# Key masks moved to ScalarE, bfloat16 counts and a reordered turn 1 in a fused attention and expert kernel

## The chip, the cores and the metric

The kernel runs on one core of one Trainium2 chip. The metric is the device time of one execution in microseconds (us); lower is better. Before the change the kernel takes 670.79 us (median of three runs: 670.62, 670.79 and 671.94).

## What is computed

Clustered attention comes first, then a layer of experts on its output. A query sees only the keys of its own cluster, and every token goes to one expert.

```python
# q, k, v: (4 batches, 8 heads, 768 tokens, 64), float32; centroids: (8, 16, 64)
q_assign = argmax(q_n @ c_n.T)            # nearest of 16 centroids, per head
k_assign = argmax(k_n @ c_n.T)
mask     = q_assign[..., :, None] == k_assign[..., None, :]
scores   = where(mask, q @ k.T / 8, -1e9)
x        = softmax(scores) @ v            # reshaped to (3072, 512)
logits   = x @ w_gate                     # 8 experts
e        = argmax(logits);  g = softmax(logits)[e]
out      = g * (relu(x @ w1[e]) @ w2[e])  # w1: 512x1024, w2: 1024x512 per expert
```

## The kernel before

**Attention.** The work is cut into 16 pairs of heads, numbered 0 to 15 (`NPAIR`, four pairs for each batch). Within a pair, `score` (L384) runs for 2 halves of the queries times 6 tiles of 128 keys, 12 score tiles in all. Each score tile is one product of keys and queries and one product of the masks `MK` and `MQ` in bfloat16 (L379), accumulated in the same bank of PSUM, and then one exponential on ScalarE (L392). The mask product adds a huge number where key and query have the same cluster, and takes it away elsewhere. After all 12 tiles, `attend` (L400) multiplies the exponentials by v (L404), 24 product instructions, and ScalarE copies the two halves of the result out (`oT`, L411). VectorE adds up the exponentials (`acc`, L398).

The masks of pair n+1 are made during pair n by `prepare` (L469), in steps: `similar` (step 1) is the product with the centroids; `assign0`, `assign1` (step 2) and `assign2` (step 3) find the cluster on VectorE and end with a transposition into `ohT` (L348); `place` (L350) writes the masks. `place(n, 1)` is step 4 and makes the key mask `mk` from `ohT` with four VectorE instructions of 32 partitions x 384 (L361: times ksc2, plus kscn2, which are columns of 128 partitions); `place(n, 0)` is step 5 and makes the query mask `mq` with four ScalarE copies of the same shape (L359). `MK` and `MQ` have two buffers each, used alternately; the `ohT` buffer is single. The first pair's masks (n = 0) are made ahead of the loop.

What happens when is an order written out by hand. `at_pair(n, u, f)` (L771) queues a step after score tile u of pair n; u = 0 to 11 follow the score tiles, u = 12 and 13 follow the two halves of the product with v. Line 779 has the steps' places:

```python
for u, step in ((2 if n else 4, 1), (5, 2), (7, 3), (8, 4), (11, 5)):
    at_pair(n, u, prepare, n + 1, step)
```

In the trace each engine works through its instructions in the order of this code, so a step that waits on VectorE holds up every later VectorE step.

**Routing.** For each batch, `gate`, `choose`, `count` and `number` (L490 to L560) find each token's expert and its place in that expert's list. `count` (L535) is two TensorE products of 128x128 float32 weights (`lt_strict`, L539, and `ones_sq`, L540) with the 8 columns `last`. GpSimd writes the tokens to their places in `tokens_of` in DRAM (L554). The routing of the last batch runs inside expert turn 0.

**Experts.** There are 10 turns, numbered 0 to 9 (`EARLY` and `RANKED`, L28), each of 128 to 448 tokens of one expert. For turn s: `places(s)` (L653) reads a register and loads the tokens' places into `sf` by SyncE's DMA queue; `indices(s)` (L669) turns them into row numbers `gi` on VectorE; `gather(s)` (L678) fetches the rows `xg` by GpSimd; `weigh(s)` (L691, tile `xw`) multiplies them by weights on VectorE and writes them to DRAM; `take(s)` (L712, tile `xs`) reads them back in another arrangement; `turn_rows(s)` (L723, tile `xT`) transposes them. `layer1` (L895) and `layer2` (L999) multiply by w1 and w2 in seven products per block instead of eight (a Strassen-Winograd scheme), so VectorE makes sums of operands first: `x_sums` (tile `xc`), `w1_sums` (tiles `a0` to `a3`), `w2_sums` (tiles `v0` to `v3`), `h_sums` (tile `hs`). All of these sums go through `strassen`, so the profile has them on one line, L736. In `layer1` VectorE also adds two PSUM results (`add`, L874), and the last product of each half has to wait until the first of these additions has read its bank.

Inside a turn, `hook()` is called after each product, and `at(h1, i, f)` or `at(h2, i, f)` queues a step at hook i of layer 1 (hooks 0 to 6 belong to the first half of the columns, 7 to 13 to the second) or layer 2. Lines 1134 to 1182 hold this order. In turn 1, before the change, layer 1 has: hook 4, `indices(3)`, `gather(3)` and v1; hook 6, `weigh(2)` and then v3; hook 9, a2 of turn 2; hook 10, a1 of turn 2; and only after that the addition L874 of the second half. `ask` and `answer` (L622, L632) check the softmax sums once, in turn 3. SyncE issues nearly all DMAs of these turns from one queue, in order.

Of the kernel before, what the change touches and what calls it, by code (L numbers as in the profile page):

```python
# [8 lines left out]
F32 = mybir.dt.float32  # L9
# [24 lines left out]
def kernel(  # L34
# [11 lines left out]
    nc = tc.nc  # L46
# [73 lines left out]
    sums = rte.tile([P, NPAIR, HI], F32)  # L120

    lt_strict = consts.tile([P, P], F32)
    keep = consts.tile([P, E, TC], F32)
    ones_sq = consts.tile([P, P], F32)
    none = consts.tile([P, NPL // P, TR], F32)
# [11 lines left out]
    def routing_constants():  # L137
        nc.gpsimd.memset(none, float(NONE))
        nc.gpsimd.memset(none[:, :, 1:TR], 0.0)
        for e in range(E):  # L140
            nc.sync.dma_start(
                out=t_d[e * NPL : (e + 1) * NPL].rearrange("(p c) o -> p (c o)", p=P), in_=none.rearrange("p c o -> p (c o)")
            )
        nc.gpsimd.memset(lt_strict, 1.0)
        nc.gpsimd.affine_select(
            lt_strict, lt_strict, compare_op=ALU.is_gt, fill=0.0, base=0, pattern=[[1, P]], channel_multiplier=-1,
        )
        nc.gpsimd.memset(ones_sq, 1.0)
        nc.gpsimd.memset(keep, 1.0)
        nc.gpsimd.memset(keep[:, :, 0:1], 0.0)  # L150
        nc.gpsimd.memset(tg, 0.0)
        tok_a = iota("tok_a", [Q4, B, NQ, 4], [[S, B], [1, NQ], [S // 4, 4]], 0, NQ).rearrange("t b j a -> t b (j a)")
        for g in range(4):
            nc.gpsimd.tensor_copy(tg[Q4 * g : Q4 * (g + 1), :, :, 0], tok_a[:, :, TC * g : TC * (g + 1)])
        nc.gpsimd.memset(caps, 0.0)
        nc.gpsimd.memset(ranks, 0.0)
        for w, (cs, rs) in enumerate(((EARLY, range(len(EARLY))), (RANKED, RANKS))):
            for i, (c, r) in enumerate(zip(cs, rs)):
                nc.gpsimd.memset(caps[:, w, i : i + 1], float(c))
                nc.gpsimd.memset(ranks[:, w, i : i + 1], float(r))  # L160
        nc.gpsimd.tensor_copy(run, first_place)

    with tc.manual_schedule(), ExitStack() as actx:
# [186 lines left out]
        def place(n, w):  # L350
            t, m = OH[n], (MQ, MK)[w][n % 2]
            for h in range(2):
                for a in range(2):
                    g = 2 * w + h
                    dst = m[D * a : D * a + Q4, HS * h : HS * (h + 1)]
                    src = t[Q4 * g : Q4 * (g + 1), :]
                    if w == 0:

                        (nc.gpsimd.tensor_copy if n == 0 and h else nc.scalar.copy)(dst, src)  # L359
                    else:  # L360
                        nc.vector.tensor_scalar(  # L361
                            dst, src, scalar1=ksc2[Q4 * g : Q4 * (g + 1), a : a + 1],
                            scalar2=kscn2[Q4 * g : Q4 * (g + 1), a : a + 1], op0=ALU.mult, op1=ALU.add,
                        )
            if w == 0:
                OH.pop(n)

# [143 lines left out]
        def choose(b):  # L511

            lg = LG.pop(b)
            sc = rt.tile([P, TC, E], F32, name="sc")
            nc.vector.tensor_tensor(sc, lg, LMAX.pop(b).unsqueeze(2).to_broadcast([P, TC, E]), op=ALU.is_ge)
            nc.vector.scalar_tensor_tensor(
                sc, in0=sc, scalar=float(2 * E), in1=first_e[:, None, :].to_broadcast([P, TC, E]),
                op0=ALU.mult, op1=ALU.add,
            )
            mx2 = rt.tile([P, TC], F32, name="mx2")  # L520
            nc.vector.reduce_max(mx2, sc, axis=AX)
            sel = SEL[b] = rt.tile([P, E, TC], F32, name="sel")
            nc.vector.tensor_tensor(
                sel.rearrange("p e t -> p t e"), sc, mx2.unsqueeze(2).to_broadcast([P, TC, E]), op=ALU.is_equal,
            )
            pr = PR[b] = rt.tile([P, E, TC], F32, name="pr")
            nc.vector.tensor_tensor_scan(
                pr.rearrange("p e t -> p (e t)"), keep.rearrange("p e t -> p (e t)"),
                sel.rearrange("p e t -> p (e t)"), 0.0, op0=ALU.mult, op1=ALU.add,
            )  # L530

            last = LAST[b] = rt.tile([P, E], F32, name="last")
            nc.vector.tensor_copy(last, pr[:, :, TC - 1])

        def count(b):  # L535

            last = LAST.pop(b)
            cps = CPS[b] = BANK.pop()[:, 2 * P : 4 * P] if BANK else ps_m.tile([P, 512], F32, name="mps")
            nc.tensor.matmul(cps[:, 0:E], lhsT=lt_strict, rhs=last, start=True, stop=True)  # L539
            nc.tensor.matmul(cps[:, E : 2 * E], lhsT=ones_sq, rhs=last, start=True, stop=True)  # L540

        def number(b):
            pr, sel, cps = PR.pop(b), SEL.pop(b), CPS.pop(b)
# [194 lines left out]
        def x_sums(s):  # L738
            g = GR[s]
            b11, b12, b21, b22 = g["X"]  # L740
            n = g["T"]
            xc = xp.tile([P, 4 * T_MAX], F32, name="xc")
            X = [xc[:, i * n : (i + 1) * n].rearrange("p (b t) -> p b t", b=2) for i in range(4)]
            V = nc.vector
            strassen(V, X[0], b12, b11, ALU.subtract)
            strassen(V, X[1], b22, X[0], ALU.subtract)
            strassen(V, X[2], b22, b12, ALU.subtract)
            strassen(V, X[3], b21, X[1], ALU.subtract)
            g["XS"] = X

# [23 lines left out]
        for n in range(NPAIR):  # L774
            if n:
                at_pair(n, 2, sum_up, n - 1)
                at_pair(n, 4, rows, n - 1)
                at_pair(n, 4, store, n - 1)
            for u, step in ((2 if n else 4, 1), (5, 2), (7, 3), (8, 4), (11, 5)):
                at_pair(n, u, prepare, n + 1, step)  # L780
        for b in range(B - 1):
            n = HP * (b + 1)
# [59 lines left out]
    with tc.manual_schedule(), ExitStack() as ectx:  # L842
# [5 lines left out]
        seeded = pool("seeded", 3, space=PSUM)  # L848
        for _ in range(3):
            nc.tensor.matmul(  # L850
                seeded.tile([P, 512], F32, name="sbank"), lhsT=ones_sq.bitcast(BF16)[:, 0:P],
                rhs=first_cb[:, None, :].to_broadcast([P, 512 // C, C]), start=True, stop=True,
            )
        wb = pool("weights_b", 1)
# [261 lines left out]
        for s in range(NS):  # L1116
# [5 lines left out]
            if s == 0:  # L1122
                at(h1, 2, sum_up, n - 1)
                at(h1, 2, weights_of, n - 1)
                at(h1, 3, gate, B - 1)
                at(h1, 3, gate_exp, B - 1)
                at(h1, 5, gate_sum, B - 1)
                at(h1, 5, choose, B - 1)
                at(h1, 8, count, B - 1)
                at(h1, 9, number, B - 1)  # L1130
                at(h1, 11, rows, n - 1)
                at(h1, 11, store, n - 1)
                at(h1, 12, rank_all)
                at(h2, 0, rank_rest)
                at(h2, 3, places, 2)
                at(h2, 3, first_weights, 2)
                at(h2, 7, indices, 2)
                at(h2, 7, gather, 2)
            if s == 3:
                at(h1, 5, ask)  # L1140
                at(h1, 9, answer)
            if s < last:
                if 2 < s + 2 <= last:
                    places(s + 2)
                if s == 0:
                    first_weights(1)
                elif s > 1:
                    take(s + 1)
                if s == 1:
                    at(h1, 6, weigh, 2)  # L1150
                    at(h1, 7, take, 2)
                    at(h1, 8, second_weights, 2)
                else:
                    second_weights(s + 1)
                if 0 < s <= last - 2:
                    at(h2, 0, first_weights, s + 2)

                if s == 0:
                    when = ((h2, 1), (h2, 2), (h2, 4), (h2, 5), (h2, 7), (h2, 7))
                elif s == 1:  # L1160
                    when = ((h1, 9), (h1, 10), (h2, 2), (h2, 3), (h2, 6), (h2, 6))
                else:
                    when = ((h1, 9), (h1, 10), (h2, 1), (h2, 2), (h2, 2), (h2, 5))
                if GR[s + 1]["T"] >= 2 * P:
                    for (h, i), f, a in zip(when, (w1_sums,) * 4 + (w2_sums,) * 2, (2, 1, 0, 3, 2, 0)):
                        at(h, i, f, s + 1, (a,), nc.vector)
                at(h2, 1 if s == 1 else 3, turn_rows, s + 1)
                if GR[s + 1]["T"] >= 2 * P:
                    at(h2, 1 if s == 1 else 4, x_sums, s + 1)
# [9 lines left out]
                at(h2, 6 if s == 1 else 4, weigh, s + 2)  # L1179
            if pairs_of(s):  # L1180
                at(h1, 4, w2_sums, s, (1,), nc.vector)
                at(h1, 6, w2_sums, s, (3,), nc.vector)
            if s == last - 1:

                at(h1, 4, nc.gpsimd.drain)
# [274 lines left out]
```

## Time and profile before

The profile is of one execution, which took 672.25 us; the traced span is 670.7 us of it, and 1.6 us lie around it.

| what | value |
|---|---|
| median of three runs | 670.79 us |
| profiled execution, its span | 672.25 us, 670.7 us |
| TensorE busy (matmul) | 649.9 us, 97% of the span |
| VectorE busy | 512.3 us, 76% |
| ScalarE busy | 300.0 us, 45% |
| GpSimd busy | 127.3 us, 19% |
| mean granted TensorE clock | 0.992 of full speed |
| attention, pairs 0 to 15 | from the start to 336.5 us |
| expert turns 0 to 9 | 336.5 us to the end |

In the profile PE is TensorE's matmul, PEld its weight load, DVE VectorE, ACT ScalarE, POOL GpSimd and SP SyncE. A row of the timeline gives start and length in us, engine, line, operation, tile written and tiles read, shape and count, and in brackets how long the engine was idle before it and what released it. A row of the waits gives the waiting engine and line, the releasing engine and line, the total wait in us, how often, and the longest.

### The profile page before, as it was taken

The page shows a single profiled execution, that of the slowest core. Times are in us where ns is not written, and L with a number is a line of the kernel's source. Part 1 is how long each engine was busy: PE and PEld are TensorE (multiplying, and loading weights), DVE is VectorE, ACT ScalarE, POOL GpSimd, SP SyncE. Part 2 cuts the span into 40 slices and gives each one's busy share as a digit, 9 for nine tenths or more (in the row PEclk, how much of TensorE's full clock was granted, in tenths as well). Part 3 has the DMA queues.
Part 4 walks back from the last instruction along what each step waited for, and adds up shares of the span by engine and source line. Part 5 has one row for each costly group of instructions (what it writes and reads, how often), then busy time and mean ns, then how long its engine had stood idle before and what let it go on. Part 6 is the DMA issues. An engine that isn't in the chain of part 4 may idle for free.

```text
span 670.7 us, 11366 instructions
## 1 busy us (share of the span) xinstructions
PE 649.9 (97%) x4210; PEld 425.7 (63%) x4210; DVE 512.3 (76%) x901; ACT 300.0 (45%) x522; POOL 127.3 (19%) x156
## 2 busy tenths in 40 slices
PE   5999999999999999999999999999999999999995
PEld 2444444454444455444575879989798887969773
DVE  5889999999999999999886868878778366572300
ACT  3666556657556565556622333243332331423210
POOL 4100000012000300033104704225240422130010
PEclk9899999999999999999999989999999999999998
DMA  6843455433455443347475586685675844625010
GB/s 118 191 86 72 82 95 95 66 73 72 77 95 95 65 81 73 70 115 239 115 266 142 189 297 217 253 321 156 275 239 229 261 160 138 221 93 182 8 48 18
DMA packets 191806, 95.36 MB, mean 142 GB/s; under 512 B 155967, under 2 KB 173887, under 8 KB 190464
## 3 DMA queue, kind: packets, MB, share of 16 engines
q1 hardware_dynamic: 184560, 81.15, 44.0%
q0 software_dynamic: 4928, 12.97, 5.8%
q8 instruction: 35, 0.57, 0.4%
q10 hardware_dynamic: 2256, 0.44, 0.4%
q14 instruction: 27, 0.22, 0.1%
HBM read 74.10 MB, written 20.70 MB: 141 GB/s over the span
## 4 chain that ended last, share of the span: by engine, by line
PE 77%; issue 9%; DVE 7%; POOL 2%; DMA 2%; ACT 1%; POOLq 0%; SPq 0%; DVEq 0%; ACTq 0%
PE sps L379 20%; PE mps L404 15%; PE bank L916 9%; PE sbank L916 7%; PE bank L1017 7%; PE bank L1036 7%; PE sbank L1017 5%; PE mps L427 2%; PE mps L312 2%; DMA xg<-x_rows,gi 1%; PE bank L885 1%; DVE acc L398 1%; DVE v L736 1%; DVE xT L727 1%; POOL tokens_of L554 1%
## 5 line engine op out<-in xcount | busy, mean ns | idle before, releaser
L392 ACT ACTIVATE A<-sps 128x768 f32<-128x768 f32 x192 | 153.5, 811 | 44.9 <-PE sps L379 44.1
L379 PE MATMUL sps<-qT,kT 64*128 64x384 f32 x768 | 159.3, 494 | 0.6 <-ACT A L392 0.6
L398 DVE TENSOR_TENSOR acc<-acc,A 128x768 f32<-128x768 f32 x128 | 121.4, 948 | 10.1 <-ACT A L392 2.8
L404 PE MATMUL mps<-A,v_in 128*64 128x384 f32 x768 | 127.4, 488 | 0.0
L379 PEld LDWEIGHTS sps<-qT,kT 64*128 64x128 f32 x768 | 67.1, 188 | 55.0 <-issue 51.4
L404 PEld LDWEIGHTS mps<-A,v_in 128*64 128x64 f32 x768 | 53.8, 137 | 70.5 <-issue 61.7
L991 POOL DMA_INDIRECT out_dram<-z,si x30 | 47.6, 1587 | 198.4 <-DVE z L874 169.3
L554 POOL DMA_INDIRECT tokens_of<-tg,pos_i x24 | 26.7, 1111 | 281.9 <-DVE pos_i L552 148.2
L379 PE MATMUL sps<-mq,mk 64*128 64x384 bf16 x384 | 63.5, 325 | 2.6 <-DVE mk L361 2.6
L1036 PE MATMUL bank<-w,h 128*128 128x512 f32 (+2 forms) x224 | 64.4, 596 | 0.0
L685 POOL DMA_INDIRECT xg<-x_rows,gi x30 | 42.7, 1423 | 48.2 <-DVE si L676 18.1
L359 ACT COPY mq<-ohT 32x384 bf16<-32x384 bf16 x62 | 31.6, 510 | 42.7 <-DVE ohT L348 41.8
L916 PE MATMUL sbank<-xc,a 128*128 128x144 f32 (+4 forms) x288 | 48.0, 310 | 0.2
L916 PE MATMUL bank<-xT,w 128*128 128x144 f32 (+4 forms) x288 | 47.8, 309 | 0.0
L874 DVE TENSOR_TENSOR h<-sbank,p 128x288 f32<-128x288 f32 (+4 forms) x18 | 9.2, 512 | 48.3 <-PE sbank L916 48.3
L916 PEld LDWEIGHTS bank<-xT,w 128*128 128x128 f32 x288 | 43.8, 191 | 2.6 <-issue 2.2
L1036 PEld LDWEIGHTS bank<-w,h 128*128 128x128 f32 (+2 forms) x224 | 24.7, 152 | 32.5 <-issue 32.3
L916 PEld LDWEIGHTS sbank<-xc,a 128*128 128x128 f32 x288 | 43.3, 191 | 0.9 <-ACT sbank L940 0.6
L379 PEld LDWEIGHTS <-mk 64*128 64x128 bf16 x384 | 19.5, 95 | 28.0 <-DVE mk L361 3.4
L934 ACT ACTIVATE h<-h 128x288 f32<-128x288 f32 (+4 forms) x36 | 17.6, 488 | 42.7 <-DVE h L874 42.5
L702 DVE TENSOR_TENSOR xw<-xg,sf 128x256 f32<-128x256 f32 (+2 forms) x60 | 32.8, 606 | 1.8 <-DMA xg<-x_rows,gi 1.6
L398 DVE TENSOR_TENSOR acc<-A 128x768 f32<-128x768 f32 x32 | 30.2, 945 | 3.1 <-ACT A L392 2.9
(208 smaller groups left out, 890.7 us busy)
## 6 DMA issues: line engine op xcount, KB each, us to landing
w<-in_moe_w_dram SPq DMA_DIRECT2D x20, 2048.0 KB, 12.0
v_in<-in_v_dram SPq DMA_DIRECT2D x32, 192.0 KB, 2.8
x_rows<-x SPq DMA_DIRECT2D x64, 96.0 KB, 2.4
turn_rows<-xw SPq DMA_DIRECT2D x23, 256.0 KB, 2.0
q_in<-in_q_dram SPq DMA_DIRECT2D x60, 96.0 KB, 3.2
k_in<-in_k_dram SPq DMA_DIRECT2D x60, 96.0 KB, 3.2
xs<-turn_rows SPq DMA_DIRECT2D x16, 144.0 KB, 2.8
xs<-turn_rows SPq DMA_DIRECT2D x8, 208.0 KB, 4.2
```

The lines of the kernel that those rows point to most:

```text
L359: (nc.gpsimd.tensor_copy if n == 0 and h else nc.scalar.copy)(dst, src)
L379: nc.tensor.matmul(SP[n, h, j][:, a, 0:HS], lhsT=kt[rows, j * P : (j + 1) * P], rhs=qt[rows, h * HS : (h + 1) * HS], start=first, stop=not ...
L392: nc.scalar.activation(A[n, h, j], ps[:, :, 0:HS], AF.Exp, scale=D**-0.5)
L398: nc.vector.tensor_tensor(ACC[n, h], first, A[n, h, j], op=ALU.add)
L404: nc.tensor.matmul(O[n, h][D * a : D * (a + 1), 0:HS], lhsT=VIN[n][:, a, j, :], rhs=A[n, h, j][:, a, :], start=(j == 0), stop=(j == NQ - 1),)
L554: ins = nc.gpsimd.indirect_dma_start(out=t_d[:, :], out_offset=bass.IndirectOffsetOnAxis(ap=pos_i[:, i : i + 1], axis=0), in_=tg[:, b, i, ...
L685: nc.gpsimd.indirect_dma_start(out=xg[0:m], out_offset=None, in_=x_d[0:rows_in, :], in_offset=bass.IndirectOffsetOnAxis(ap=g["gi"][0:m, j ...
L702: nc.vector.tensor_tensor(xw[0:m, :, :, d2 * a : d2 * (a + 1)], xg[0:m].rearrange("p (r a d b) -> p a r b d", r=HP, a=2, b=DB)[:, a], g["s ...
L916: nc.tensor.matmul(ps[:, f * T2 : (f + 1) * T2], lhsT=w[:, k, (2 * j + f) * P : (2 * j + f + 1) * P], rhs=x[:, k, :], start=first and f + ...
L991: ins = nc.gpsimd.indirect_dma_start(out=out[:, :], out_offset=bass.IndirectOffsetOnAxis(ap=GR[s]["si"][0:rows, j : j + 1], axis=0), in_=z ...
L1017: nc.tensor.matmul(ps[:, 0:H], lhsT=x[:, k, :], rhs=y[:, k, :], start=first and k == 0, stop=k == 3, skip_group_check=not first,)
L1036: nc.tensor.matmul(ps[i * m : (i + 1) * m, :], lhsT=h[:, f, j * P : j * P + m], rhs=w[:, f, :], start=(k == 0), stop=(k == FB // n - 1),)
```

## The change

There are five edits.

1. **Key masks.** For every pair but the first, `mk` is made by four ScalarE activations (function Identity, with scale and bias as columns) in place of the four VectorE instructions, and step 4 moves from score tile 8 to score tile 11. ScalarE's queue at the end of a pair is then: twelve exponentials, four `mk`, four `mq`, two `oT`.
2. **Counts.** `last` is bfloat16, and the weights of `count` are bfloat16 copies, made once by GpSimd at the start. The three products that prime the seeded banks (L850) use the bfloat16 ones too.
3. **Places.** `places(s + 3)` is issued in turn s, layer 2, hook 1, in place of `places(s + 2)` at the start of turn s; the first ones are set by hand. On SyncE's queue it now stands ahead of the writes of `weigh(s + 2)` rather than behind them. For turn 3 the queue's order is unchanged.
4. **Order in turns 0 and 1.** In turn 0, a0 and a3 of turn 1 come one hook later, so the four `xc` sums of turn 1 come first. In every `x_sums`, the third sum (X[2], which the second product needs) is made first. In turn 1, v3 goes from hook 6, behind `weigh(2)`, to hook 5, ahead of it; a1 goes from hook 10 to hook 12, behind both additions L874 of the second half.
5. **The check of the sums.** In turn 3, `ask` goes from layer 1, hook 5, to hook 12, and `answer` from layer 1, hook 9, to layer 2, hook 4.

```diff
+    lt_b = consts.tile([P, P], BF16)
+    ones_b = consts.tile([P, P], BF16)
...
+        nc.gpsimd.tensor_copy(lt_b, lt_strict)
+        nc.gpsimd.memset(ones_b, 1.0)
...
-                        nc.vector.tensor_scalar(
-                            dst, src, scalar1=ksc2[Q4 * g : Q4 * (g + 1), a : a + 1],
-                            scalar2=kscn2[Q4 * g : Q4 * (g + 1), a : a + 1], op0=ALU.mult, op1=ALU.add,
-                        )
+                        big, less = (t[Q4 * g : Q4 * (g + 1), a : a + 1] for t in (ksc2, kscn2))
+                        if n == 0:
+                            nc.vector.tensor_scalar(dst, src, scalar1=big, scalar2=less, op0=ALU.mult, op1=ALU.add)
+                        else:
+                            nc.scalar.activation(dst, src, AF.Identity, bias=less, scale=big)
...
-            last = LAST[b] = rt.tile([P, E], F32, name="last")
+            last = LAST[b] = rt.tile([P, E], BF16, name="last")
...
-            nc.tensor.matmul(cps[:, 0:E], lhsT=lt_strict, rhs=last, start=True, stop=True)
-            nc.tensor.matmul(cps[:, E : 2 * E], lhsT=ones_sq, rhs=last, start=True, stop=True)
+            nc.tensor.matmul(cps[:, 0:E], lhsT=lt_b, rhs=last, start=True, stop=True)
+            nc.tensor.matmul(cps[:, E : 2 * E], lhsT=ones_b, rhs=last, start=True, stop=True)
...
+            strassen(V, X[2], b22, b12, ALU.subtract)
             strassen(V, X[0], b12, b11, ALU.subtract)
             strassen(V, X[1], b22, X[0], ALU.subtract)
-            strassen(V, X[2], b22, b12, ALU.subtract)
             strassen(V, X[3], b21, X[1], ALU.subtract)
...
-            for u, step in ((2 if n else 4, 1), (5, 2), (7, 3), (8, 4), (11, 5)):
+            for u, step in ((2 if n else 4, 1), (5, 2), (7, 3), (11, 4), (11, 5)):
...
-                seeded.tile([P, 512], F32, name="sbank"), lhsT=ones_sq.bitcast(BF16)[:, 0:P],
+                seeded.tile([P, 512], F32, name="sbank"), lhsT=ones_b,
...
+                at(h2, 5, places, 3)
...
             if s == 3:
-                at(h1, 5, ask)
-                at(h1, 9, answer)
+                at(h1, 12, ask)
+                at(h2, 4, answer)
             if s < last:
-                if 2 < s + 2 <= last:
-                    places(s + 2)
...
+                if 0 < s <= last - 3:
+                    at(h2, 1, places, s + 3)
...
                 if s == 0:
-                    when = ((h2, 1), (h2, 2), (h2, 4), (h2, 5), (h2, 7), (h2, 7))
+                    when = ((h2, 1), (h2, 2), (h2, 5), (h2, 6), (h2, 7), (h2, 7))
                 elif s == 1:
-                    when = ((h1, 9), (h1, 10), (h2, 2), (h2, 3), (h2, 6), (h2, 6))
+                    when = ((h1, 9), (h1, 12), (h2, 2), (h2, 3), (h2, 6), (h2, 6))
...
-                at(h1, 6, w2_sums, s, (3,), nc.vector)
+
+                at(h1, 5 if s == 1 else 6, w2_sums, s, (3,), nc.vector)
```

## The prediction

> **What bounds the kernel.** TensorE: 97% of the span is matmul and the granted clock is 0.992. So I read first who TensorE waits for, then the stretches around the long waits. The list of TensorE's waits:
>
> ```profile
> PE sbank L916 <- DVE h L874: 3.4, 3, 2.4
> PE sps L379 <- DVE mk L361: 2.6, 2, 2.4
> PE mps L427 <- DVE acc L398: 0.9, 2, 0.7
> PE sbank L1017 <- DVE z L874: 0.6, 2, 0.4
> PE bank L916 <- DVE xc L736: 0.2, 1, 0.2
> PE mps L539 <- DVE last L533: 0.2, 1, 0.2
> ```
>
> The reader is to see that almost nothing can be won: all waits after the start add up to some 5.5 us. The mk wait (2.6) is at the very start (15.4 to 16 us), for pair 0, whose masks the change leaves on VectorE; it stays. The largest (2.4) sits in turn 1. TensorE's and VectorE's timelines there:
>
> ```profile
> 383.06 1.15 PE L916 MATMUL bank<-xc,w 128*128 128x144 f32 x8
> 386.62 2.27 PE L916 MATMUL sbank<-xT,a 128*128 128x144 f32 x8 [2.42 <-DVE h L874]
> ```
>
> ```profile
> 378.25 0.44 DVE L874 TENSOR_TENSOR h<-bank,u 128x288 f32<-128x288 f32 x1
> 379.31 1.14 DVE L702 TENSOR_TENSOR xw<-xg,sf 128x256 f32<-128x256 f32 x2 [0.63 <-DMA xg<-x_rows,gi]
> 381.45 1.15 DVE L702 TENSOR_TENSOR xw<-xg,sf 128x256 f32<-128x256 f32 x2 [0.99 <-DMA xg<-x_rows,gi]
> 382.52 1.21 DVE L736 TENSOR_TENSOR v<-w,v 128x1024 f32<-128x1024 f32 x1
> 383.65 1.22 DVE L736 TENSOR_TENSOR a<-w 128x1024 f32<-128x1024 f32 x1
> 384.97 1.23 DVE L736 TENSOR_TENSOR a<-w,a 128x1024 f32<-128x1024 f32 x1
> 386.11 0.45 DVE L874 TENSOR_TENSOR h<-sbank,p 128x288 f32<-128x288 f32 x1
> ```
>
> VectorE idles 1.6 us for gathered rows, makes three sums that nobody needs yet, and only then does the addition that TensorE has needed since 384.20. The product after it takes 2.27 us where its neighbour takes 1.15. The table by stretches says why (TensorE's clock is the 0.50 before the DMA share):
>
> ```profile
> 386.70:390.10 3.40, 3.40 (x12) 3.13 (x13) 1.20 (x3) 1.48 (x4) 0.00 (x0) 0.50 0.78 206
> ```
>
> So this wait costs 2.42 us and then half of 3.4 us, 1.7 us.
>
> The other place that matters is the end of pair 13 (timeline of all engines):
>
> ```profile
> 293.31 0.58 DVE L348 STREAM_TRANSPOSE ohT<-oh 128x384 bf16<-128x384 bf16 x1
> 293.93 2.10 ACT L359 COPY mq<-ohT 32x384 bf16<-32x384 bf16 x4 [5.24 <-DVE ohT L348]
> 294.77 1.58 DVE L361 TENSOR_SCALAR mk<-ohT,ksc,kscn 32x384 bf16<-32x384 bf16 x4
> 296.41 0.33 PE L379 MATMUL sps<-mq,mk 64*128 64x384 bf16 x2
> 299.51 0.68 PE L427 MATMUL mps<-acc,ones_s 128*32 128x192 f32 x10 [0.71 <-DVE acc L398]
> ```
>
> From ohT's end (293.89) to pair 14's first mask product (296.41) there are 2.5 us. Read in the same way, it is 6.0 us in an ordinary pair (pair 2: 69.64 to 75.63) and 4.6 us in the tightest other ones (pairs 6 and 10). Pair 13 is late because VectorE also does the routing there.
>
> **The Trainium skill.** "TensorE: Matmul & The Clock Gate", section "What's actually happening": the clock falls to half after an idle window, and windows are free-running, 3413 ns long. The trace agrees on half and on the length. A 2.4 us wait was enough here; waits up to 0.71 us were not. "ScalarE: Activation LUTs", section "What ACT_TABLE_LOAD costs": an activation takes 186 ns + 0.833 ns per element, about 93 ns more per column operand, and neighbours overlap by about 93 ns. The trace's L392 with 768 elements (811 ns against 826) agrees; no row here has two column operands. The same page, "Table sets: the hidden batching unit", has identity in every table set, so exponentials and masks can alternate without a load; no run shows that yet, but the changed program's instruction list has the same two table loads as before.
>
> **Key masks on ScalarE.** Removed from VectorE: 15 x 1.58 = 24 us, worth only what TensorE waited for it. Added to ScalarE: 15 x 4 activations. Price: between 0.43 us (the f32 row L934, 0.44 us at 288 elements, carried to 384, less the overlap) and 0.70 us (186 + 2x93 + 320 by the skill's figures, no overlap); I take 0.60. Four are 2.4 us, then the mq copies, 0.53 us apart. Queued behind them are two oT copies and the next pair's exponentials. TensorE's first mask products need the first two mq copies: 0.04 + 2.4 + 1.06 = 3.5 us after ohT. With 6.0 or 4.6 us there, nothing shows: ScalarE's whole tail (2.4 + 2.1 + 0.9 = 5.4 us) lies beside the product with v (7.9 us) and the three score tiles that have buffers. In pair 13 only 2.5 us are there: a new wait of 1.0 us (0.3 with the low price, 1.4 with the high one). In return VectorE's addition is done 1.6 us sooner, and the wait of 0.71 at 299.51 goes. Net +0.3 us. What is late next: nothing; exponentials start at about 299.4, and TensorE's fourth score tile comes after 301.
>
> VectorE stays some 1.6 us ahead into turn 0. There the waits of 0.17 (L427), 0.41 (L916 for h) and 0.20 (L539) come from its backlog (w1 sums until 343.7 us), so they go: -0.8 us.
>
> **Counts.** A count takes 0.54 us of TensorE (138.76 to the next product at 139.30): four f32 passes with weight loads of 0.19 us. A 128x8 bf16 product is in no row; the 64x128 bf16 load takes 0.095 us. Two products with two loads should need 0.25 to 0.3 us. Bounds: no gain, or 0.4 each. I take 0.25, four times: -1.0 us. The two extra GpSimd instructions (0.2 to 0.3 us each, like L144 and L145) end long before turn 0 uses GpSimd; the priming products stay bf16: nothing.
>
> **Turn 1.** X[2] first: the wait of 0.23 for xc goes. Before the addition: v3 now runs from 378.6 to 379.8, in the time spent waiting for rows; the first rows' xw ends at 380.9; the second rows land at 381.4 as before (gather(2) hangs on gi, which follows the same sum of VectorE work), so xw ends at 382.5; a2 until 383.65; addition done at 384.1. TensorE wants it at 384.20, or 383.97 with xc's wait gone: 0.15 us is left of 2.42. With so short a wait the clock should stay up: 1.7 us more. a1 (1.2 us) lies in VectorE's idle time before h_sums. But the layer 2 that follows is entered 4 us sooner, and VectorE still has a1, hs, the three z additions, xT, xc, a0 and a3, some 13 us, before the z addition that TensorE's last product needs: I count 0.25 us of new wait. Sum: -0.23 - 2.27 - 1.7 + 0.25 = -3.95 us.
>
> **The check.** In turn 3 the 2.5 us of okm, of waiting for L635 (0.79 us) and of the small instructions stand ahead of a2, a1 and the addition; TensorE waits 0.55 us. At hook 12, okm (0.9 us) fits into VectorE's 0.81 us of idle time before hs; answer's five (0.8 us) delay xw and a z addition that no product waits for, and the next turn's first addition has 0.9 us of idle time ahead of it. L635 only changes place. -0.55 us.
>
> **Places.** VectorE waits 1.7 us in all for sf; in turn 4 this ends in some 0.1 us of TensorE. On SyncE the register load and one or two issues (0.4 us each) now run ahead of DMAs that wait for weigh anyway, and take, w2 and later DMAs move up by that. Only sf's four buffers could hold it back, and the one reused was last read two turns ago. -0.1 us.
>
> **Sum:** +0.3 - 0.8 - 1.0 - 3.95 - 0.55 - 0.1 = -6.1 us. Against the profiled 672.25: 666.15. The runs' median is 1.46 us lower. If that is an offset of profiling, the median becomes 664.7; if it is the half-clock stretch, which free-running windows needn't give in every run, part of the gain isn't in the median, and it becomes about 666.1. I take 665.3.
>
> **Rivals.** (a) Turn 1's wait stays: the rows land later than 381.4, because 2 MB of weights are loading beside them, or the clock falls all the same. For it: VectorE waited for these rows twice, and GpSimd's issue took 2.92 us. Against: gather and load keep their order. Then 3.7 of the 3.95 us are lost: 669.0. (b) Slower: the mask queue at the pair's end becomes the bound. It has 3.5 us of work ahead of the first mask product at 0.60 us per activation. At 1.05 us each it is 5.3 us: the six pairs with 4.6 to 5.1 us (5, 6, 9, 10, 12, 14) lose 1.9 together, pair 13 loses 2.7 and falls to half clock (1.7): 6.3 in all, less 0.7, and the gain elsewhere (6.4) is nearly eaten. At 1.2 us: 5.5 + 3.3 + 1.7 - 0.7 - 6.4 = +3.4, so 674.2. For it: no row has such an activation. Against: the skill's price is 0.70 at most. (c) The pieces shrink: counts bring nothing, pair 13 waits 1.4 us and its window falls to half clock: 665.3 + 1.0 + 0.4 + 1.7 = 668.4.
>
> **Chances.** Forecast 0.66 (663.3 to 667.2: low mask price and 0.4 per count, to no gain from counts and high mask price); (a) 0.15; (c) 0.13; (b) 0.06. Range 663.2 to 669.0, which leaves out (b) and half of (a). A measurement can tell about 0.2%, 1.3 us: below 669.4 is faster. Half of (a) may land within: faster 0.85, same 0.09, slower 0.06.
>
> **What would show it.** Right: no wait of TensorE over 0.3 us near 380, clock 1.00 through turn 1; none at 441; one of about 1 us before pair 14's first mask product, released by mq; count records halved; sf waits gone. Wrong: mk activations over 0.8 us, TensorE waiting for mq in more pairs than one, rows landing late in turn 1, or a wait moved to layer 2's z additions that is larger than 0.3 us.

## The result, and the profile after

The changed kernel takes 659.72 us (median of five runs, 659.62 to 660.34); the kernel before, beside it, 671.49 us (670.62 to 672.79). The ratio is 0.9828 (95% interval 0.9814 to 0.9841), 11.8 us less. The forecast was 665.3 us (663.2 to 669.0), from 6.1 us less than the profiled run. The direction was right, the size was about half of what came, and 659.72 lies below the range.

The profiled execution took 659.62 us, its span 657.8 us; the clock was 0.995 of full speed. I read the two traces stage by stage, by the start of each stage's first product:

| stage | forecast, us | measured, us |
|---|---|---|
| start and attention (masks +0.3, three counts -0.75) | -0.45 | -4.2 |
| turn 0 (backlog -0.8, one count -0.25) | -1.05 | -2.5 |
| turn 1, both layers | -3.95 | -4.5 |
| turn 3 (the check) | -0.55 | -0.8 |
| turns 2, 4 and 5 (places) | -0.1 | -0.4 |
| after the last product | 0 | -0.4 |
| sum | -6.1 | -12.8 |

The profiled executions differ by 12.6 us, the medians by 11.8.

The waits of TensorE after the change (us in total, times, longest), without the two at the start:

```profile
PE sps L385 <- ACT mq L364: 1.0, 2, 0.8
PE sbank L1023 <- DVE z L880: 0.7, 3, 0.4
PE sps L385 <- ACT A L398: 0.6, 1, 0.6
```

The waits for h (turn 1), acc and xc are gone. One is new: mq, 1.0 us, in pair 14 as forecast. These lists differ by some 3 us, and the time by 12. So most of the gain isn't in the list that the forecast was made from.

Turn 1 after the change, VectorE and then TensorE:

```profile
371.77 1.20 DVE L742 TENSOR_TENSOR v<-w,v 128x1024 f32<-128x1024 f32 x1
372.91 2.17 DVE L708 TENSOR_TENSOR xw<-xg,sf 128x256 f32<-128x256 f32 x4
375.00 1.20 DVE L742 TENSOR_TENSOR a<-w 128x1024 f32<-128x1024 f32 x1
376.39 0.46 DVE L880 TENSOR_TENSOR h<-sbank,p 128x288 f32<-128x288 f32 x1 [0.19 <-PE sbank L922]
```

```profile
377.10 1.15 PE L922 MATMUL sbank<-xT,a 128*128 128x144 f32 x8
```

v3 comes first, the rows are there, a2 follows, and now the addition waits for TensorE (0.19 us). The product takes 1.15 us, not 2.27: no stall and no half clock.

The masks on ScalarE, by the page's groups (busy us, mean ns, then idle time ahead):

```profile
L370 ACT ACTIVATE mk<-ohT,kscn,ksc 32x384 bf16<-32x384 bf16 x60 | 42.0, 700 | 37.4 <-DVE ohT L353 36.6
```

700 ns each: the upper bound of the forecast, and close to the estimate of 692 ns that the Trainium skill's figures give without overlap ("ScalarE: Activation LUTs", "What ACT_TABLE_LOAD costs"). The page has neighbours overlap by about 93 ns; the four of a pair take 2.85 us, so these don't. Masks and exponentials alternate without a table load: the profile has two ACT_TABLE_LOADs, at 2.6 and 4.1 us, the same as before.

Where did attention's 4.2 us come from? An ordinary pair takes 11.85 us from its first score product to its first product with v, before and after. Pairs 6 and 10 took 12.93 and now take 11.99 and 11.98; pair 13 took 13.53, now 11.99; pair 14 13.84, now 13.34. In pair 6 no wait of TensorE is listed at all. Its timeline before, behind the third score tile (VectorE's kT, then TensorE):

```profile
137.00 0.94 DVE L277 STREAM_TRANSPOSE kT<-k_in 128x768 f32<-128x768 f32 x1
137.47 0.81 PE L312 MATMUL mps<-qT,cT 128*32 128x384 f32 x4
137.99 0.84 PE L312 MATMUL mps<-kT,cT 128*32 128x384 f32 x4
138.76 0.39 PE L539 MATMUL mps<-last,lt_strict 128*128 128x8 f32 x2
```

and after:

```profile
137.24 0.49 PE L317 MATMUL mps<-qT,cT 128*32 128x384 f32 x2
137.26 0.49 PE L317 MATMUL mps<-kT,cT 128*32 128x384 f32 x2
...
138.00 0.18 PE L545 MATMUL mps<-last,lt_b 128*128 128x8 bf16 x1
...
138.14 0.92 PE L385 MATMUL sps<-qT,kT 64*128 64x384 f32 x4
```

`similar` is four products that fill 32 columns of the array each, two of them on qT and two on kT. After, all four run side by side (qT and kT start 0.02 us apart), and the count begins 0.76 us after the first. Before, kT's pair begins 0.52 us after qT's, because VectorE's transposition into kT is late: it ends at 137.94, and kT's products begin at 137.99. The same instructions take 1.29 us, and TensorE counts as busy throughout. This fits the Trainium skill ("TensorE: Matmul & The Clock Gate", "The mechanism"): products on different tiles of the array run together, and they start and end strictly in program order. The trace agrees: 0.02 us apart when all operands are there, and with kT late the count stays behind kT's pair. The count itself takes 0.14 us in place of 0.54.

In the kernel before, the lateness of kT stands only in the waits of the weight loads:

```profile
PEld mps L312 <- DVE kT L277: 2.4, 4, 0.9
PEld mps L427 <- DVE acc L398: 1.9, 3, 1.1
```

And VectorE's own waits for exponentials tell how full it was, first before, then after:

```profile
DVE acc L398 <- ACT A L392: 5.8, 15, 1.1
```

```profile
DVE acc L404 <- ACT A L398: 23.6, 24, 2.6
```

In all of attention VectorE's additions waited only 5.8 us for them. The page's 76% is an average: from pair 1 to the end of attention VectorE was busy 279.4 of 301.4 us, 93%, and after the change 87%.

### The profile page after: what moved, and what is told of

Same layout as the page of the kernel before. It is cut to its first block, busy times and chain, and to the rows that moved or that the text cites. A ratio compares the mean times of both kernels' runs of the same rounds, so it can differ in the third digit from the quotient of the medians.

```text
span 657.8 us, 11371 instructions
## 1 busy us (share of the span) xinstructions
PE 640.8 (97%) x4202; PEld 421.6 (64%) x4202; DVE 490.4 (75%) x841; ACT 338.8 (52%) x582; POOL 126.1 (19%) x158
## 4 chain that ended last, share of the span: by engine, by line
PE 85%; DVE 10%; DMA 1%; ACT 1%; issue 1%; SPq 0%; POOL 0%; POOLq 0%; DVEq 0%; ACTq 0%
PE sps L385 20%; PE mps L410 16%; PE bank L922 12%; PE bank L1042 10%; PE sbank L922 9%; PE bank L1023 7%; PE sbank L1023 6%; DVE acc L404 3%; PE mps L433 2%; PE mps L317 2%; DVE a L742 1%; PE bank L891 1%; DVE xT L733 1%; DMA q_in<-in_q_dram 1%; DVE v L742 1%
## 5 line engine op out<-in xcount | busy, mean ns | idle before, releaser
L370 ACT ACTIVATE mk<-ohT,kscn,ksc 32x384 bf16<-32x384 bf16 x60 | 42.0, 700 | 37.4 <-DVE ohT L353 36.6
L691 POOL DMA_INDIRECT xg<-x_rows,gi x30 | 40.3, 1343 | 46.9 <-DVE si L682 16.4
```

The lines of the kernel that those rows point to most:

```text
L370: nc.scalar.activation(dst, src, AF.Identity, bias=less, scale=big)
L691: nc.gpsimd.indirect_dma_start(out=xg[0:m], out_offset=None, in_=x_d[0:rows_in, :], in_offset=bass.IndirectOffsetOnAxis(ap=g["gi"][0:m, j ...
```

## The experiments

Every kernel computes the whole result. Ratios are against the kernel before, run in the same group (672.14, 671.89 and 671.66 us). In the first four, the two theories are: backlog (the masks took VectorE's time, so operands came late and TensorE ran slowly while it counted as busy) and count (the gain of the count pairs lies in the counts).

**Masks alone.** Edit 1 on the kernel before:

```diff
-                        nc.vector.tensor_scalar(
-                            dst, src, scalar1=ksc2[Q4 * g : Q4 * (g + 1), a : a + 1],
-                            scalar2=kscn2[Q4 * g : Q4 * (g + 1), a : a + 1], op0=ALU.mult, op1=ALU.add,
-                        )
+                        big, less = (t[Q4 * g : Q4 * (g + 1), a : a + 1] for t in (ksc2, kscn2))
+                        if n == 0:
+                            nc.vector.tensor_scalar(dst, src, scalar1=big, scalar2=less, op0=ALU.mult, op1=ALU.add)
+                        else:
+                            nc.scalar.activation(dst, src, AF.Identity, bias=less, scale=big)
...
-            for u, step in ((2 if n else 4, 1), (5, 2), (7, 3), (8, 4), (11, 5)):
+            for u, step in ((2 if n else 4, 1), (5, 2), (7, 3), (11, 4), (11, 5)):
```

> The kernel before with the first edit alone: the key masks of pairs 1 to 15 on ScalarE at score tile 11. Backlog theory (VectorE's lateness slows TensorE in ways that the list of matmul waits doesn't show, because four products of 32 columns that could run abreast run in twos): pair 6 from its first score to its product with v goes from 12.93 to 12.4 us, pair 13 from 13.53 to about 12.4, pair 14 keeps a wait of 1.0 us on the query masks, turn 0's layer 1 loses about 2 us of 17.9; in all 3.5 to 4.5 us faster. Count theory (the f32 counts are what slows these pairs): pair 6 stays at 12.9 us, and the whole gain is under 1 us.

Measured: 0.9937 (0.9923 to 0.9951), 4.2 us less. Pairs 6, 10 and 13 take 12.39 us each: an ordinary pair (11.85) and an old count (0.54). Pair 14 takes 13.32 with its 1.0 us of waiting. Pair 6 behind its third score tile:

```profile
137.92 0.49 PE L312 MATMUL mps<-qT,cT 128*32 128x384 f32 x2
137.93 0.49 PE L312 MATMUL mps<-kT,cT 128*32 128x384 f32 x2
...
138.68 0.39 PE L540 MATMUL mps<-last,lt_strict 128*128 128x8 f32 x2
```

With the old count, the four products run side by side again. In the profile the four pairs are 2.7 us shorter and turn 0's layer 1 is 2.05 us shorter; the forecast had -0.5 in all. The stall of 2.50 us in turn 1 stays, but this time the clock doesn't fall after it.

Not all of the 2.05 us need be the masks'. Late in pair 15 VectorE waits for turn 0's rows. Before the change:

```profile
330.27 1.38 DVE L727 STREAM_TRANSPOSE xT<-xs 128x1152 f32<-128x1152 f32 x1 [2.11 <-DMA xs<-turn_rows]
```

This wait varies, and turn 0's layer 1 with it. With all masks still on VectorE it is 2.11 us (layer 1: 17.90 us) here, 2.70 to 3.10 (18.17 to 18.39) with edit 4, with edits 3 and 5 and in the first try below, but 1.31 (16.21, of which the count gained 0.4) with the counts alone and 1.36 (16.69) in the second try below. With the masks alone it is 1.02 (15.85). Where the waits are nearly alike, 1.36 and 1.02 us, layer 1 differs by 0.84 us: an estimate of the masks' own part, and about what the forecast had for turn 0. So in the profile the masks are worth between 3.6 and 4.8 us. Why the rows land sooner or later is open.

**Counts alone.** Edit 2 on the kernel before:

```diff
-            last = LAST[b] = rt.tile([P, E], F32, name="last")
+            last = LAST[b] = rt.tile([P, E], BF16, name="last")
...
-            nc.tensor.matmul(cps[:, 0:E], lhsT=lt_strict, rhs=last, start=True, stop=True)
+            nc.tensor.matmul(cps[:, 0:E], lhsT=lt_b, rhs=last, start=True, stop=True)
...
```

and the other lines of the edit (the bfloat16 weights, the second product, the priming products).

> The kernel before with the second edit alone: counts and their weights in bfloat16. Backlog theory: each count gives back 0.4 us (0.54 to 0.14 us from its first product to the next one), pair 6 goes from 12.93 to 12.5 us, in all 1.2 to 1.6 us faster. Count theory: pair 6 goes to 12.0 us as in the changed kernel, in all 3 to 4 us faster.

Measured: 0.9965 (0.9949 to 0.9981), 2.35 us less. Pairs 6, 10 and 13 take 12.52, 12.53 and 13.12 us, 0.40 less each: the count, and nothing of the lateness. The next pairs, 7 and 11, take 0.16 and 0.18 us longer. Four counts at 0.40 us are 1.6 us, which lies within the interval (1.3 to 3.4 us).

**Order alone.** Edit 4 on the kernel before:

```diff
-                    when = ((h1, 9), (h1, 10), (h2, 2), (h2, 3), (h2, 6), (h2, 6))
+                    when = ((h1, 9), (h1, 12), (h2, 2), (h2, 3), (h2, 6), (h2, 6))
...
-                at(h1, 6, w2_sums, s, (3,), nc.vector)
+                at(h1, 5 if s == 1 else 6, w2_sums, s, (3,), nc.vector)
```

and the two other lines of the edit (X[2] first, a0 and a3 a hook later).

> The kernel before with the fourth edit alone: the order of VectorE's sums in turns 0 and 1. If the wait of 2.4 us in turn 1 and the half clock behind it go for this reason, turn 1 (both layers) goes from 33.0 to about 28.5 us and the clock stays 1.00 there: 4.3 us faster. If the gathered rows land too late without VectorE's gain from the masks, a wait of over 1 us is left in turn 1 and the gain is under 2 us.

Measured: 0.9946 (0.9934 to 0.9959), 3.6 us less. In the profile turn 1's layer 1 is 4.13 us shorter and its layer 2 0.58; the stall is gone, and a wait of 0.155 us comes in layer 2.

**The rest alone.** Edits 3 and 5 on the kernel before:

```diff
-                at(h1, 5, ask)
-                at(h1, 9, answer)
+                at(h1, 12, ask)
+                at(h2, 4, answer)
...
-                if 2 < s + 2 <= last:
-                    places(s + 2)
...
+                if 0 < s <= last - 3:
+                    at(h2, 1, places, s + 3)
```

> The kernel before with the third and fifth edits alone: places loaded a turn sooner, and the check of the sums moved out of turn 3's first layer. If each gives what the changed kernel shows in turns 3 to 5 (layer 1 of turn 3 from 14.8 to 13.7 us, of turn 4 by 0.25, of turn 5 by 0.35, less 0.45 given back in the second layers), 1.2 us faster. If those gains need the time that VectorE is ahead because of the other edits, nothing.

Measured: 0.9977 (0.9964 to 0.9989), 1.5 us less. In the profile turn 3 is 0.7 us shorter (-1.05 in layer 1, +0.32 in layer 2), turn 4 0.25 and turn 5 0.36. By the ratios the four gains add up to 11.65 us, and the change brings 11.8. Each gain is known to about 1 us, and within that the parts don't depend on each other.

**Is it the order of VectorE's queue, or its load?** The first try, on the kernel before:

```diff
-            at_pair(n + (not last), 10 if last else 9, choose, b)
+            at_pair(n + (not last), 10 if last else 13, choose, b)
-            at_pair(n + 2 - last, 2, count, b)
-            at_pair(n + 2 - last, 3 if last else 6, number, b)
+            at_pair(n + 2 - last, 2 if last else 6, count, b)
+            at_pair(n + 2 - last, 3 if last else 9, number, b)
```

> The kernel before with one thing moved: choose (six small VectorE instructions, 1.35 us) comes after the next pair's qT and kT instead of ahead of them, at hook 13, and count and number three hooks later to suit; the last round's (pair 13) stay. No work leaves VectorE or TensorE, and the masks stay on VectorE. Late-operand theory: what the masks cost in pairs 6 and 10 was only that kT came after qT's products had begun, so that the four 32-column products ran two and two; kT is now 1.35 us earlier (136.6 instead of 138.0), the four run together, and pairs 6 and 10 take 12.4 us instead of 12.93, as they did with the masks alone; pair 13 stays at 13.5; some 1.0 us in all (ratio about 0.9985). Rival (load): VectorE's work slows TensorE by being there, whatever its order, for instance through shared reads; then pairs 6 and 10 stay at 12.9 and the time stays within 0.3 us of before.

Measured: 1.0145 (1.0112 to 1.0177), 10 us longer. Both theories missed this: `number` now frees count's PSUM bank so late that the products with v wait for it, 2.85 us in pairs 6 and 10 each, and each time half clock follows. The part that was meant to be tested is seen all the same: pair 6's four products run side by side and its scores take 12.59 us, not 12.93.

The second try leaves count and number in place, so that only VectorE's queue changes:

```diff
-            at_pair(n + (not last), 10 if last else 9, choose, b)
+            at_pair(n + (not last), 10 if last else 13, choose, b)
```

> The kernel before with only VectorE's queue changed: choose comes after the next pair's qT and kT, as in the run with choose moved late, but count and number stay in their places, so that TensorE's instructions and their order are those of before. Late-operand theory: kT is ready 1.35 us earlier, the four 32-column products run together again, pairs 6 and 10 take 12.4 us (12.93 before) while count still costs its 0.54, and no wait for run is left: some 1.0 us less than before in all, as much as taking 24 us of masks from VectorE gave there. Rival (load): pairs 6 and 10 stay at 12.9 because VectorE has as much to do as before.

Measured: 1.0012 (0.9994 to 1.003), no gain. Pairs 6 and 10 take 12.40 and 12.39 us as the late-operand theory said, with all the masks still on VectorE. But the lateness comes back in the next pairs. Whole pairs 6, 7 and 8 of this kernel, and then pairs 6 to 8 of the kernel before (stretch, its length, then busy us of PE, PEld, DVE, ACT and POOL with instruction counts, clock, DMA):

```profile
134.76:155.05 20.29, 20.29 (x159) 10.18 (x157) 19.21 (x41) 12.36 (x18) 4.77 (x5) 1.00 0.45 83
155.05:175.51 20.46, 20.46 (x155) 9.80 (x153) 18.27 (x30) 12.33 (x18) 2.02 (x2) 1.00 0.40 74
175.51:195.58 20.07, 20.07 (x154) 9.78 (x153) 19.06 (x33) 12.16 (x17) 0.00 (x0) 1.00 0.47 84
```

```profile
133.84:154.66 20.82, 20.82 (x159) 10.33 (x157) 19.64 (x38) 12.36 (x18) 5.28 (x5) 1.00 0.46 83
154.66:174.41 19.75, 19.75 (x154) 9.67 (x152) 18.77 (x31) 12.64 (x18) 1.50 (x2) 1.00 0.44 81
174.41:194.15 19.74, 19.74 (x154) 9.70 (x152) 18.52 (x32) 12.16 (x17) 0.00 (x0) 1.00 0.43 80
```

60.82 us against 60.31: pair 6 wins 0.53, pairs 7 and 8 lose 0.71 and 0.33. In these lines VectorE is busy 89 to 95% and TensorE 100%. The weight loads' waits for kT say the same: 2.4 us in all before, 2.2 with this order, 0.9 with the masks alone. So late operands are how TensorE is slowed (first theory), and VectorE's load is why they are late (the rival): this other order only picks the pair that pays, less work takes the cost away.

**The change once more**, nothing edited, for the three that follow.

> The changed kernel once more, nothing edited, to compare the others of this group with it on the same chip: ratio 0.982 to 0.984.

Measured: 0.9818 (0.9788 to 0.9847), 660.01 us. In this profile turn 3 is 1.26 us longer than in the first one of the same kernel, as ScalarE and VectorE start 0.9 us late on one product's result. Three later profiles (a1 back, pair 14 split, and the masks doubled) have 0.5 to 0.8 us of this; its cause stays open.

**Turn 1: v3 put back behind weigh.**

```diff
-                at(h1, 5 if s == 1 else 6, w2_sums, s, (3,), nc.vector)
+                at(h1, 6, w2_sums, s, (3,), nc.vector)
```

> The changed kernel with v3 (one sum of 1.2 us) put back behind weigh in turn 1; the other three moves of that turn stay. My theory (order): the addition h comes 1.2 us later than TensorE wants it, less what slack there is: a wait of 1.0 to 1.3 us before turn 1's second half, and 1.0 to 1.3 us longer than the change if the clock stays up (about 1.2 us of idle time is half of what halved it before); 1.7 more in a profile whose clock falls. Rival (rows): the wait is set by the gathered rows, not by the sums; then v3 fits into that idle time either way and nothing shows.

Measured: 0.9823 (0.9794 to 0.9853), 660.18 us; turn 1 isn't longer, and the addition comes at 376.56 with no wait of TensorE. The rival is right. The rows are no longer late: GpSimd's first two gather instructions take 1.79 and 0.96 us here, in the change and with the order alone, but 2.92 and 2.02 to 2.03 us in the six profiles with the old order in turn 1.

**Turn 1: a1 put back ahead of the addition.**

```diff
-                    when = ((h1, 9), (h1, 12), (h2, 2), (h2, 3), (h2, 6), (h2, 6))
+                    when = ((h1, 9), (h1, 10), (h2, 2), (h2, 3), (h2, 6), (h2, 6))
```

> The changed kernel with a1 (one sum of 1.2 us) put back ahead of the addition h in turn 1, v3 and the rest as changed. My theory (order): with rows that are there when weigh begins, the addition ends 1.0 to 1.2 us later than TensorE wants it: a wait of 1.0 us there and in layer 2 up to 0.15 us back; a wait of 1 us leaves the clock up. If the rows land late as before, 1.0 to 2.0. Rival: as with v3, the sum fits into idle time and nothing shows.

Measured: 0.9825 (0.9801 to 0.9848), 660.81 us. In the profile the wait is back, 0.70 us. At full clock, turn 1's layer 1 takes 14.69 us, against 13.93 in the first profile of the change and 13.72 in the second:

```profile
377.50 1.25 PE L922 MATMUL sbank<-xT,a 128*128 128x144 f32 x8 [0.70 <-DVE h L880]
```

My theory, with 0.70 in place of 1.0. In the old order a1, the late rows and v3 behind them together made 2.42.

**Pair 14's wait: masks by halves.**

```diff
             elif step == 4:
-                place(n, 1)
+                if n == 0:
+                    place(n, 1)
+            elif n == 0:
+                place(n, 0)
             else:
-                place(n, 0)
+                for h in range(2):
+                    place(n, 1, (h,))
+                    place(n, 0, (h,))
```

`place` takes the halves as a third argument here: two `mk` and two `mq` of the first half, then of the second.

> The changed kernel with ScalarE's eight mask instructions of a pair in the order of the halves that the first products read: mk and mq of half 0 (two each), then of half 1. My theory: pair 14's first mask product then waits for two mk and two mq (2 x 0.72 + 2 x 0.53 = 2.5 us after ohT instead of 3.9), so its wait of 1.0 us falls to 0 to 0.2 us and the kernel is 0.8 to 1.0 us faster than the change, some 658.8. Rival: the products of key tile 0 need only half 0 of mk, but the wait is on the last of the eight all the same, or the second half is late by as much a little later (key tiles 3 to 5, within 2.5 us): then the wait stays at 0.8 to 1.0 or moves by some products, and the time is the change's within 0.2 us.

Measured: 0.9817 (0.9788 to 0.9846), 659.86 us, the change's time. The wait for mq is gone, but three score tiles later sum_up waits 1.05 us for the copy oT, which stands behind the masks in ScalarE's queue. Pair 14 takes 13.02 us, not 13.34: the rival, nearly. The rows came as late here as in the old order (gather 2.92 and 1.48 us; xw waits 0.63), and TensorE waited no more than 0.04 us in turn 1's layer 1: there the moves of v3 and a1 make up for the late rows. Which of the two is needed for that is not shown; no run has late rows and one of them put back.

**Pair 14's wait: half of the masks on VectorE.**

```diff
...
-                        if n == 0:
+                        if n == 0 or (n == NPAIR - 2 and h == 0):
...
                 assign2(n)
+                if n == NPAIR - 2:
+                    place(n, 1, (0,))
...
-                place(n, 1)
+                place(n, 1, (1,) if n == NPAIR - 2 else (0, 1))
```

> The changed kernel, but for pair 14 alone half of the key masks (two instructions, 0.8 us) are made by VectorE right after ohT, and ScalarE makes the other two. Theory: the wait of 1.0 us at pair 14 is the length of ScalarE's whole queue in pair 13 (masks, copies, oT), so two activations less (1.43 us) take it away wherever it shows, and VectorE's two instructions fit: its last addition ends 0.8 us later, about when sum_up wants it. Pair 14 then starts 0.75 to 0.9 us after its first product as elsewhere, no wait over 0.3 us at sum_up, 0.7 to 1.0 us less than the change. Rival: the addition acc is late by the 0.8 us instead, and the time is the change's within 0.2.

Measured: 0.9828 (0.9805 to 0.9852), 660.67 us. No wait over 0.1 us is left in pair 14, and yet it takes 13.26 us. VectorE was full, so acc, qT and kT are late again, much as the rival said:

```profile
295.80 0.84 PE L317 MATMUL mps<-qT,cT 128*32 128x384 f32 x4
296.56 0.84 PE L317 MATMUL mps<-kT,cT 128*32 128x384 f32 x4
297.33 0.92 PE L385 MATMUL sps<-qT,kT 64*128 64x384 f32 x4
```

1.53 us for the four products, where the change takes 0.76. The waiting became busy time: the list of waits looks better and the time is the same.

**The slower rival: the mask queue doubled.**

```diff
-                            nc.scalar.activation(dst, src, AF.Identity, bias=less, scale=big)
+                            for _ in range(2):
+                                nc.scalar.activation(dst, src, AF.Identity, bias=less, scale=big)
```

Each activation is done twice with the same values.

> The changed kernel with every key-mask activation on ScalarE done twice (the same values; 8 instead of 4 per pair), 42 us more work for an engine that is busy 52%. The forecast's slower rival, its price doubled: the first mask product then comes 8 x 0.72 + 1.06 = 6.8 us after ohT. Slack is 6.0 us in an ordinary pair, 4.6 in pairs 5, 6, 9, 10 and 12, less in pair 13. If the queue decides: waits of 0.8 us in seven or eight ordinary pairs, about 2 in five, some 4 before pair 14: 20 us or more longer than the change. If the exponentials' buffers hide more than I think: waits only before pair 14, 3 to 4 us longer.

Measured: 1.0436 (1.0413 to 1.0459), 701.93 us, 42 us longer than the change, twice the least that was expected.

```profile
PE sps L386 <- ACT mq L364: 21.3, 28, 3.7
```

All 15 pairs wait now at their first mask product, 0.4 to 3.65 us each; eight stretches of half clock follow, about 1.7 us each. The rival's mechanism is real: at 2 x 0.70 us per mask the queue at the pair's end is the bound. At 0.70 it is so only in pair 14.

## Why the prediction was wrong

- **The step that failed:** "Removed from VectorE: 15 x 1.58 = 24 us, worth only what TensorE waited for it", from "all waits after the start add up to some 5.5 us" and "almost nothing can be won". With the backlog it counted -0.5 us for edit 1; alone, the edit brings 4.2 us (0.9937). In its profile pairs 6, 10, 13 and 14 are 2.7 us shorter, where the forecast had them 0.3 longer. In turn 0 it had 0.8 less, and 0.8 to 2.05 came. What VectorE cost TensorE was mostly no wait but products running two at a time instead of four: 0.54 us in pairs 6 and 10 each, 1.14 in pair 13, where the forecast had none of it. Two ways of making kT earlier (masks alone; choose behind kT) both gave 12.4 us, and VectorE's load decides whether that lasts.
- **New wait at pair 14:** right in place and releaser; that the list has just the 1.0 us of the forecast is luck. The activation took 0.700 us, not 0.60, and for 0.70 the forecast had 1.4:

```profile
293.66 0.32 PE L385 MATMUL sps<-mq,mk 64*128 64x384 bf16 x1 [0.79 <-ACT mq L364]
294.19 0.32 PE L385 MATMUL sps<-mq,mk 64*128 64x384 bf16 x1 [0.21 <-ACT mq L364]
```

TensorE was free at 292.87 and begins the second of these two products at 294.19, so the delay is 1.3 us; 0.32 of it counts as busy under the first product. The low price, 0.43, took off an overlap of neighbours; the four mq copies in the forecast's own lines (2.10 us; 510 ns each in the profile before) already showed none.
- **A reading that was off:** an ordinary pair has 5.7 us from ohT to the first mask product (69.64 to 75.37), not 6.0. It changes nothing in the sum.
- **"What is late next: nothing":** right for the waits, but oT stands next in ScalarE's queue (1.05 us when the masks are made by halves).
- **Counts:** mechanism right, size off: 0.40 us each, not 0.25. The records took 0.17 us and overlap (0.04 us from one to the next), so two products take 0.14.
- **Turn 1:** right in sum, 4.5 us against 3.95, of which the clock is 1.7, but in part by luck, since the rows came sooner than it counted on. Inside it, "the second rows land at 381.4 as before" was wrong: xw finds its rows without a wait. So of the two moved sums only a1's move counts in the profile of the change (0.70 us); v3's move would matter with late rows, which is not shown. The new wait in layer 2 was 0.155 us, for 0.25.
- **The check and the places:** right in direction, 1.2 us together in the profile for 0.65.
- **Profile and median:** the doubt was right. The half clock is in some executions and not in others (next section but one), which fits the profiled 672.25 being 1.46 us above the median; the varying wait for turn 0's rows can add to it. The changed kernel has no such stall, and its five runs lie within 0.7 us.
- **Rivals:** (a) and (c) didn't come: turn 1's wait and its half clock are gone, and the counts did gain. (b) is a real mechanism, but its point, 1.05 us per activation, is far above 0.700; at twice 0.700 it cost 42 us.

## What to carry to other kernels

That TensorE is busy isn't proof that it is fast: compare the same group of products in an ordinary and in a busy stretch, and read the waits of the weight loads beside those of the matmuls. Before an engine is called idle, take its busy share in the stage in question, not over the span; on an engine that is full there, less work is worth something, and another order, in the one that was tried here, wasn't. When a wait is taken away, look at the length of the stage and not at the list of waits.

## What the runs showed of the hardware

**Half clock goes by a fixed grid.** The stretches at half clock are 3.41 us long, or twice that, and all of a run lie on one grid of 3.41 us. In 14 profiles, their first 23 and last 20 us aside, each stretch of the grid in which TensorE was idle for 1.77 us or more (up to 2.85; 10 cases) was followed by one at half clock, and none with up to 1.24 us. Between 1.64 and 1.72 us, about half of the stretch, four were and three weren't. So a stall of 2.5 us costs 1.7 us more or nothing more, by where the grid cuts it. Before the change 2.42 us fell into one stretch; with the masks alone 2.50 us was cut by the grid into 0.83 and 1.67. In the same columns as above, the stretch with the stall in the kernel before (the next one, at clock 0.50, stands in the prediction), and then that stretch and the next with the masks alone:

```profile
383.27:386.68 3.41, 0.99 (x9) 0.78 (x7) 3.19 (x4) 0.08 (x1) 2.04 (x2) 1.00 0.69 235
```

```profile
380.48:383.89 3.41, 1.74 (x12) 1.67 (x13) 2.05 (x3) 1.24 (x4) 0.67 (x1) 1.00 0.77 166
383.89:387.31 3.42, 3.42 (x24) 1.55 (x23) 2.68 (x4) 0.86 (x3) 0.00 (x0) 1.00 0.83 204
```

The busy time of TensorE is the number behind the length: 0.99 of 3.41 us led to clock 0.50, 1.74 of 3.41 us to 1.00.

The Trainium skill ("TensorE: Matmul & The Clock Gate", "What's actually happening") has the free-running window of this length, and an idle window of about 3.4 us as the condition; here about half a window of idleness was enough.

**A gather instruction's length varies.** GpSimd's first gather for turn 2 takes 1.79 us in seven profiles and 2.92 us in seven, though it starts 0.3 us into the same VectorE sums of v (2.35 us) in all fourteen. The six with the old order in turn 1 and masks by halves have 2.92, the others 1.79. No run tells why.
